# Recurrence and feed-forward kernel: a block's last decay fetched by small transfers in place of four matmuls, and another priority for the bias product

## Chip, cores, metric

One core of a Trainium2 chip. The metric is the device time in microseconds (us) of one execution; several executions are taken in rounds beside executions of the kernel before on the same chip. Runs in the slow state are left out of the ratios. The profile is one execution, with times from its first instruction on.

## The reference, cut

```python
f = 1.0 / (1.0 + np.exp(-f_logit))                 # q, k, v, f_logit: (4, 8, 768, 48)
for t in range(S):
    state = f[:, :, t, :, None] * state + np.einsum('bhd,bhe->bhde', k[:, :, t], v[:, :, t])
    y[:, :, t] = np.einsum('bhd,bhde->bhe', q[:, :, t], state)
x = y.transpose(0, 2, 1, 3).reshape(3072, 384)
h = x @ w_in                                       # 384 -> 2048
out = (np.maximum(h, 0) + np.log1p(np.exp(-np.abs(h)))) @ w_out   # 2048 -> 384
```

## The kernel before

Tokens come in 24 blocks of 128; six blocks make one sequence, and a 48x48 state per head is carried between them. In a block, ScalarE turns the gates into decays accumulated from the block's start (tile `ee`, tokens on partitions), POOL scales k and q by them (`qkp`), TensorE transposes and multiplies, and POOL updates the state (`sst`). The state needs the decay of the block's **last token**, a row on partition 127, as a column with one channel per partition. Four matmuls with a one-column selector (`last`) do that turn.

The feed-forward part of one block runs beside the recurrence of later blocks. All work is a list of tasks with a guessed cost and a key; a list scheduler simulates the engines and fixes the order of instructions per engine. On the chip an engine works its own list in order: SP's 192 issues in the trace of the changed kernel stand exactly as its list has them. All loads and stores are issued by SP.

```python
LOADS = 4                                    # load buffers per tensor
def in_order(tasks, slots): ...              # per engine: of the ready tasks the one that can start
                                             # first; at equal start the one with the lower key
def load(n, i):                              # n in f, k, q, v: 128 x 8 x 48 floats in 192-byte runs
    nc.sync.dma_start(out=t, in_=...)
def a_u(i):
    ...                                      # 4 matmuls 128x96: the block's k^T v
    for p in range(NP):                      # NP = 4 pairs of heads
        nc.tensor.matmul(out=ps[:, DM + p:DM + p + 1], lhsT=ek[:, p, :], rhs=last,
                         start=True, stop=True, skip_group_check=True)
def a_tt(i):
    ...                                      # tt = k^T v (+ old state)
    nc.vector.tensor_copy(out=ec, in_=ps[:, DM:DM + NP])
def a_sn(i):                                 # POOL: new state = tt * ec, twice, one per head of a pair
    nc.gpsimd.tensor_tensor(out=sn[lo:hi, :, e0:e0 + D], in0=tt[lo:hi],
                            in1=ec[lo:hi].unsqueeze(2).to_broadcast([48, NP, D]), op=ALU.mult)
# ... the tasks (engine, guessed cost in us, needs, key):
task(("go", n, i), "SP", 0.5, [(used[n], i - LOADS)], kd, load, (n, i))
task(("ek", i), "ACT", 0.48, [("cs", i)], s + 0.1, a_ek, (i,), "ee", [("mk", i), ("mq", i), ("u", i)])
task(("eq", i), "ACT", 0.48, [("ek", i)], s + 0.2, a_eq, (i,))
task(("bias mm",), "PE", 0.65, [("sum", len(sums) - 1)], NJ + LAG - 1, bias_mm, (), "att", [("bias out",)])
```

## Time and profile before

| | before |
|---|---|
| median of three runs, us | 200.12 (199.54 to 202.39) |
| span of the profiled run, us | 197.8 |
| TensorE idle between 57 and 195 us, sum of the gaps over 0.15 us, us | 0.72 |
| one block in the late part (mean of 9), us | 7.09 |
| granted TensorE clock | 1.00 |

The lines that carry this stand in the prediction. In the slices a digit is the busy share in tenths; the chain names at each moment the work on which the end depended; a bracket after a line of a timeline gives the idle time of that engine just before the instruction and who ended it.

### The profile page before, as it was taken

How to read it: one execution, taken by the hardware profiler on the slowest of the kernel's cores; microseconds unless marked ns; L12 is line 12 of the kernel's file. 1: busy time of each engine (PE TensorE's matmuls, PEld its weight loads, DVE VectorE, ACT ScalarE, POOL GpSimd, SP SyncE). 2: the span in 40 equal slices, each digit the busy share in tenths (PEclk: the TensorE clock that was granted, in tenths of full speed). 3: DMA queues.
4: the chain of work that ended last, by engine and by line, in shares of the span. 5: the costliest groups of instructions: out<-in, count | busy, mean ns of one | idle time of the engine just before them, and what ended most of it. 6: DMA issues, size and time to landing. Idle time of an engine off the chain costs nothing.

```text
span 197.8 us, 5863 instructions
## 1 busy us (share of the span) xinstructions
PE 181.5 (92%) x2354; PEld 147.9 (75%) x2354; DVE 127.8 (65%) x295; ACT 148.5 (75%) x247; POOL 97.4 (49%) x142
## 2 busy tenths in 40 slices
PE   0568898999979999999999999999999999999993
PEld 0345797777768888887788888888888888888871
DVE  6658977526949988667558657755855865773021
ACT  4446349899679899896898797898869768676870
POOL 2268747999998662460463364254246335400000
PEclk9999999999999999999999999999999999999999
DMA  6999999999999999999977657856441101100112
GB/s 127 188 187 215 352 389 373 208 201 166 196 169 202 206 203 196 246 186 199 203 155 165 120 134 150 159 118 136 114 85 41 43 0 43 40 14 29 43 40 80
DMA packets 107035, 30.26 MB, mean 153 GB/s; under 512 B 100352, under 2 KB 105472, under 8 KB 107008
## 3 DMA queue, kind: packets, MB, share of 16 engines
q1 hardware_dynamic: 107008, 29.89, 73.4%
q8 instruction: 18, 0.29, 0.7%
q14 instruction: 9, 0.07, 0.1%
HBM read 25.17 MB, written 4.72 MB: 151 GB/s over the span
## 4 chain that ended last, share of the span: by engine, by line
PE 64%; POOL 13%; SPq 9%; DMA 8%; issue 3%; ACT 2%; DVE 0%; POOLq 0%
PE ops L367 24%; PE hh L347 24%; SPq L111 8%; POOL wsum L177 7%; DMA w<-in_moe_w_out_dram 6%; PE qkT L232 4%; PE pp L257 4%; DMA ff<-in_f_logit_dram 2%; POOL w_out_bf L162 2%; PE oo L319 2%; PE xTp L333 2%; POOL qkp L214 1%; PE uu L274 1%; SPq L148 1%; PE cs L201 1%
## 5 line engine op out<-in xcount | busy, mean ns | idle before, releaser
L347 PE MATMUL hh<-xT,w_in_bf 128*128 128x128 bf16 x1152 | 118.2, 222 | 1.7 <-ACT uexp L355 1.6
L367 PE MATMUL ops<-w_out_bf,gg 128*128 128x384 bf16 x384 | 113.7, 326 | 0.0
L347 PEld LDWEIGHTS <-w_in_bf 128*128 128x128 bf16 x1152 | 92.0, 99 | 24.1 <-issue 2.8
L355 ACT ACTIVATE uexp<-hh 128x512 f32<-128x512 f32 x96 | 56.6, 594 | 26.1 <-PE hh L347 25.4
L361 ACT ACTIVATE gg<-uexp 128x1024 bf16<-128x1024 f32 x48 | 50.7, 1057 | 1.5
L303 POOL TENSOR_TENSOR sst<-tt,ec 48x192 bf16<-48x192 f32 x40 | 20.7, 517 | 44.4 <-DVE ec L295 36.6
L367 PEld LDWEIGHTS <-gg 128*128 128x128 bf16 x384 | 36.8, 98 | 3.8
L265 DVE TENSOR_TENSOR ptm<-pp,mask 128x512 bf16<-128x512 f32 x48 | 30.9, 684 | 2.8 <-PE pp L257 2.6
L214 POOL TENSOR_TENSOR qkp<-kk,ee 128x384 bf16<-128x384 f32 x23 | 21.3, 928 | 19.8 <-ACT ee L206 14.5
L239 DVE CAST xx<-oo 128x384 bf16<-128x384 f32 x21 | 11.7, 558 | 20.5 <-PE oo L319 20.3
L218 POOL TENSOR_TENSOR qkp<-qq,ee 128x384 bf16<-128x384 f32 x24 | 22.0, 915 | 5.0 <-ACT ee L210 4.9
L239 DVE COPY qkT<-qkT 128x512 bf16<-128x512 bf16 x24 | 10.1, 422 | 19.4 <-PE qkT L232 19.4
L232 PEld LDWEIGHTS <-qkp 128*128 128x128 bf16 x192 | 13.1, 104 | 8.6 <-DVE qkp L214 5.5
L232 PE MATMUL qkT<-ident,qkp 128*128 128x128 bf16 x192 | 16.9, 234 | 2.7 <-DVE qkp L214 1.5
L375 DVE TENSOR_TENSOR osb<-ops,bias_bc 128x384 f32<-128x384 f32 x20 | 11.1, 555 | 11.4 <-PE ops L367 11.1
L193 ACT ACTIVATE ff<-ff 128x384 f32<-128x384 f32 x24 | 12.2, 514 | 7.3 <-DMA ff<-in_f_logit_dram 7.3
L257 PE MATMUL pp<-qbd,qkT 112*128 112x256 bf16 x96 | 16.8, 292 | 0.5 <-DVE qbd L248 0.2
L177 POOL TENSOR_TENSOR wsum<-wsum,w 128x384 f32<-128x384 f32 x14 | 14.7, 1048 | 0.7
L206 ACT ACTIVATE ee<-cs 128x384 bf16<-128x384 f32 x24 | 11.4, 477 | 3.8 <-PE cs L201 1.6
L223 POOL CAST vb<-vv 128x384 bf16<-128x384 f32 x24 | 12.3, 517 | 2.4 <-DMA vv<-in_v_dram 1.4
L201 PE MATMUL cs<-zz,negU 128*128 128x384 bf16 x24 | 8.5, 353 | 5.4 <-ACT zz L197 5.4
L197 ACT ACTIVATE zz<-ff 128x384 bf16<-128x384 f32 x24 | 12.4, 516 | 0.3
(49 smaller groups left out, 174.6 us busy)
## 6 DMA issues: line engine op xcount, KB each, us to landing
ff<-in_f_logit_dram SPq DMA_DIRECT2D x24, 192.0 KB, 4.3
kk<-in_k_dram SPq DMA_DIRECT2D x24, 192.0 KB, 4.3
qq<-in_q_dram SPq DMA_DIRECT2D x24, 192.0 KB, 4.5
vv<-in_v_dram SPq DMA_DIRECT2D x24, 192.0 KB, 4.4
out_dram<-osb SPq DMA_DIRECT2D x24, 192.0 KB, 2.1
w<-in_moe_w_in_dram SPq DMA_DIRECT2D x4, 768.0 KB, 8.3
w<-in_moe_w_out_dram SPq DMA_DIRECT2D x4, 768.0 KB, 13.1
```

The source lines that it names most:

```text
L177: nc.gpsimd.tensor_tensor(out=wsum, in0=wsum, in1=t[:, j, :], op=ALU.add)
L214: eng.tensor_tensor(out=qkp_bufs[i % 3][:, H:2 * H, 0:D], in0=in_t.pop(("k", i)), in1=e_bufs[i % 2][:, H:2 * H, 0:D], op=ALU.mult)
L218: nc.gpsimd.tensor_tensor(out=qkp_bufs[i % 3][:, 0:H, 0:D], in0=in_t.pop(("q", i)), in1=e_bufs[i % 2][:, 0:H, 0:D], op=ALU.mult)
L232: nc.tensor.transpose(ps[:, a * 128:(a + 1) * 128], qkp[:, a, :], ident)
L239: nc.vector.tensor_copy(out=out, in_=in_)
L257: nc.tensor.matmul(out=ps[:, u * 256:(u + 1) * 256], lhsT=qkT_t[i][0:112, NP + p, :], rhs=qbd_bufs[i % 2][0:112, p, :], start=True, stop=True,
L265: nc.vector.tensor_tensor(out=ptm_t[i][:, 4 * half:4 * half + 4, :], in0=p_ps.pop((i, half)).rearrange("p (a t) -> p a t", t=128), in1=mas ...
L303: nc.gpsimd.tensor_tensor(out=sn[lo:hi, :, e0:e0 + D], in0=tt[lo:hi], in1=ec[lo:hi].unsqueeze(2).to_broadcast([48, NP, D]), op=ALU.mult)
L347: nc.tensor.matmul(out=h_ps[i, j // 4][:, j % 4, :], lhsT=w_in_bf[:, r, j * 128:(j + 1) * 128], rhs=xT_t[i][:, r, :], start=(r == 0), stop ...
L355: nc.scalar.activation(out=u_t[i, a // 2][:, 4 * (a % 2):4 * (a % 2) + 4, :], in_=h_ps.pop((i, a)), func=AF.Exp, bias=0.0, scale=1.0)
L361: nc.scalar.activation(out=g_t[i][:, 8 * a:8 * a + 8, :], in_=u_t.pop((i, a)), func=AF.Ln, bias=0.5, scale=0.5)
L367: nc.tensor.matmul(out=o_ps[i][:, 0:DM], lhsT=g_t[i][:, j, :], rhs=w_out_bf[:, j, :], start=(j == 0), stop=(j == NJ - 1), skip_group_check ...
```

## The change

Its intent: take 64 matmuls off TensorE, the bound, and let the DMA engines (full until about 100 us, idle later) turn the row into a column: one 2-byte element per partition, four transfers per block, from block 4 on. And the bias product gets a later key, so that TensorE should not wait for POOL's sums.

```diff
+EC = 4
@@ a_u
-        for p in range(NP):
-            nc.tensor.matmul(out=ps[:, DM + p:DM + p + 1], lhsT=ek[:, p, :], rhs=last, ...)
+        if i < EC:
+            for p in range(NP):
+                nc.tensor.matmul(out=ps[:, DM + p:DM + p + 1], lhsT=ek[:, p, :], rhs=last, ...)
+    def a_ec(i):
+        ec_t[i] = work.tile([128, NP], BF16, name="ecd", tag="ecd", bufs=2)
+        row = e_bufs[i % 2][127:128, 0:H, :].rearrange("o (a b) d -> o a (b d)", b=2)
+        for p in range(NP):
+            nc.sync.dma_start(out=ec_t[i][:, p:p + 1], in_=row[:, p, :],
+                              allow_slow_non_contiguous=True)
@@ a_tt
-        nc.vector.tensor_copy(out=ec, in_=ps[:, DM:DM + NP])
+        if i < EC:
+            nc.vector.tensor_copy(out=ec, in_=ps[:, DM:DM + NP])
@@ tasks
+            if i >= EC:
+                task(("goec", i), "SP", 2.0, [("eq", i)], 0, a_ec, (i,), "ecd", [("sn", i)])
+                task(("ec", i), ("landing ec", i), 2.6, [("goec", i)], 0)
-            task(("u", i), "PE", 0.28, ...)
+            task(("u", i), "PE", 0.28 if i < EC else 0.17, ...)
-    task(("bias mm",), "PE", 0.65, [...], NJ + LAG - 1, bias_mm, ...)
+    task(("bias mm",), "PE", 0.65, [...], NJ + LAG + 8, bias_mm, ...)
```

More of the change, by code (lines that the diff above doesn't have):

```diff
@@ L224, in a_vb @@
                               in_=in_t.pop(("v", i)))
+    ec_t = {}
     qkT_ps, p_ps, u_ps, o_at, xT_ps, tt_t = {}, {}, {}, {}, {}, {}
@@ L276, in a_u @@
                              skip_group_check=True)
+        if i < EC:
+            for p in range(NP):
+                nc.tensor.matmul(out=ps[:, DM + p:DM + p + 1], lhsT=ek[:, p, :], rhs=last,
+                                 start=True, stop=True, skip_group_check=True)
+        u_ps[i] = ps
+    def a_ec(i):
+        ec_t[i] = work.tile([128, NP], BF16, name="ecd", tag="ecd", bufs=2)
+        row = e_bufs[i % 2][127:128, 0:H, :].rearrange("o (a b) d -> o a (b d)", b=2)
         for p in range(NP):
-            nc.tensor.matmul(out=ps[:, DM + p:DM + p + 1], lhsT=ek[:, p, :], rhs=last,
-                             start=True, stop=True, skip_group_check=True)
-        u_ps[i] = ps
+            nc.sync.dma_start(out=ec_t[i][:, p:p + 1], in_=row[:, p, :],
+                              allow_slow_non_contiguous=True)
     def a_tt(i):
@@ L286, in a_tt @@
         tt = work.tile([128, NP, D], FP32, name="tt", tag="tt", bufs=2)
-        ec = work.tile([128, NP], FP32, name="ec", tag="ec", bufs=2)
+        ec = ec_t.pop(i) if i >= EC else work.tile([128, NP], FP32, name="ec", tag="ec", bufs=2)
         for lo, e0 in ((0, 0), (64, D)):
@@ L423 @@
         task(("ek", i), "ACT", 0.48, [("cs", i)], s + 0.1, a_ek, (i,), "ee",
-             [("mk", i), ("mq", i), ("u", i)])
+             [("mk", i), ("mq", i), ("u", i), ("ec", i)])
         task(("eq", i), "ACT", 0.48, [("ek", i)], s + 0.2, a_eq, (i,))
@@ L443 @@
         if c < NC - 1:
-            task(("u", i), "PE", 0.28, [("vb", i), ("tr", i)], s + 12, a_u, (i,), "att",
+            if i >= EC:
+                task(("goec", i), "SP", 2.0, [("eq", i)], 0, a_ec, (i,), "ecd", [("sn", i)])
+                task(("ec", i), ("landing ec", i), 2.6, [("goec", i)], 0)
+            task(("u", i), "PE", 0.28 if i < EC else 0.17, [("vb", i), ("tr", i)], s + 12, a_u, (i,), "att",
                  [("tt", i)])
-            task(("tt", i), "DVE", 0.88, [("u", i), ("sn", i - 1) if c else None], s + 12.1,
+            task(("tt", i), "DVE", 0.88 if i < EC else 0.73, [("u", i), ("ec", i), ("sn", i - 1) if c else None], s + 12.1,
                  a_tt, (i,))
@@ L478 @@
         task(("sum", n), "POOL", 0.91, [("at", "wo", w), ("sum", n - 1)], 36 + n, add_w, (w, j))
-    task(("bias mm",), "PE", 0.65, [("sum", len(sums) - 1)], NJ + LAG - 1, bias_mm, (), "att",
+    task(("bias mm",), "PE", 0.65, [("sum", len(sums) - 1)], NJ + LAG + 8, bias_mm, (), "att",
          [("bias out",)])
@@ L485 @@
         t.frees.extend(by[n] for n in t.until if n in by)
-    slots = dict(att=4, hh=2, ops=2, zz=2, ee=2, qkp=3, vb=3, qkT=2, qbd=2, ptm=2, xx=2, xT=6, uexp=3, w32=8,
+    slots = dict(att=4, hh=2, ops=2, zz=2, ee=2, qkp=3, vb=3, qkT=2, qbd=2, ptm=2, xx=2, xT=6, ecd=2, uexp=3, w32=8,
                  gg=6, osb=6)
```

## The prediction

> **What bounds the kernel now.** I read the page from the top: engine shares, the forty slices, the chain that ended last, then the timeline around what the diff touches.
>
> ```profile
> PE 181.5 (92%) x2354; PEld 147.9 (75%) x2354; DVE 127.8 (65%) x295; ACT 148.5 (75%) x247; POOL 97.4 (49%) x142
> ...
> PE   0568898999979999999999999999999999999993
> POOL 2268747999998662460463364254246335400000
> DMA  6999999999999999999977657856441101100112
> ...
> PE 64%; POOL 13%; SPq 9%; DMA 8%; issue 3%; ACT 2%; DVE 0%; POOLq 0%
> ```
>
> The reader is to see three stages. Up to about 57 us the chain runs through the loads and then POOL, which casts weights and adds the rows of the second weight matrix (15 sums of about 1 us). From 57 us to 194.5 us TensorE is full; a slice is 4.9 us. The DMA engines are full too, but only until about 100 us. The share of matmul time alone would prove little, since matmuls overlap; what proves the stage is the timeline of TensorE: between 60 and 190 us it lists only two idle gaps:
>
> ```profile
> 92.89 0.33 PE L347 MATMUL hh<-xT,w_in_bf 128*128 128x128 bf16 x3 [0.24 <-ACT uexp L355]
> 95.22 0.33 PE L347 MATMUL hh<-xT,w_in_bf 128*128 128x128 bf16 x3 [0.48 <-ACT uexp L355]
> ```
>
> Behind these 0.72 us stands ScalarE, which just before had waited for a gate load (ff), in the stretch where the DMA engines are full:
>
> ```profile
> 91.83 0.52 ACT L193 ACTIVATE ff<-ff 128x384 f32<-128x384 f32 x1 [1.75 <-DMA ff<-in_f_logit_dram]
> ```
>
> So after 57 us a matmul removed from the order is time saved one for one, unless another engine or the loads hold that stage.
>
> **What the Trainium skill says.** (1) "TensorE: Matmul & The Clock Gate", section "Back-to-back issue gap": a matmul with 1 to 64 moving columns costs an issue floor of about 25 ns, not its latency. The trace agrees: four of the removed matmuls occupy 0.105 us, worked out below, 26 ns each, though each record is 163 to 205 ns long. (2) "DMA: Bandwidth & Descriptors", section "Anatomy of one DMA — SWDGE (gpsimd) path" (written for the other issuing path): about 2 us per transfer are fixed, mostly completion; and the engines do not wait on semaphores, the issuing sequencer does, before dispatch. The trace agrees: a store takes 2.1 us to land, and SP sits in front of stores for 60.3 us in its own list of waits. (3) Same page, section "Rules for kernel authors": a strided or non-contiguous last dimension becomes one descriptor per element. No run shows this yet; I expect 128 descriptors of 2 bytes per small transfer.
>
> **The change part by part.** *Which blocks.* There are 24 blocks, the state is carried after all but every sixth, so 20 have a decay; blocks 0 to 3 keep the old way. Sixteen change: 4, 6 to 10, 12 to 16, 18 to 22.
>
> *Removed from TensorE:* four matmuls (128x1) in each of them. The steady order of the timeline gives the cost as the distance of two starts:
>
> ```profile
> 111.43 0.33 PE L274 MATMUL uu<-vb,qkp 128*128 128x96 bf16 x4
> 111.60 0.24 PE L278 MATMUL uu<-last,ee 128*128 128x1 bf16 x4
> 111.71 0.32 PE L367 MATMUL ops<-w_out_bf,gg 128*128 128x384 bf16 x1
> ```
>
> 111.71 - 111.60 = 0.11, and other blocks give 0.10 to 0.11, so 0.105 us. 16 x 0.105 = 1.7 us. Block 4 lies before 57 us, where POOL leads; 15 blocks remain, 1.6 us. Ten of these (12 to 16, 18 to 22) come after 95 us, where nothing but TensorE counts: 1.05 us are safe. The 0.5 us of blocks 6 to 10 fall in the stretch with full DMA engines and may be lost.
>
> *Removed from VectorE:* 16 copies of 163 ns, 2.6 us, of an engine that is 65% busy and at 0% of the chain: nothing.
>
> *Added on SP and the DMA engines:* 64 transfers of 128 descriptors. A store, also of 128 descriptors, holds SP for 0.36 us when the queue is free, and the next issue can start some 0.1 us later; four of them are an estimated 1.8 us of SP per block. A block now has four loads and a store, 4 x 0.45 + 0.45 = 2.3 us of issue in a period of 7.0 us when the queue is free, so there is room late in the kernel. In the full stretch one load takes 0.98 us for 1024 descriptors, that is 64 on each of 16 engines, 15 ns each. At that rate 512 more descriptors per block are 32 x 15 ns = 0.5 us; 2-byte writes may be dearer. Blocks 4 and 6 to 10 are six blocks, 3 us of additional queue before 95 us, or more if SP's waiting holds the loads up.
>
> *Does the value arrive in time?* The state update on POOL (sst) reads it. In the steady state of block 14:
>
> ```profile
> 107.71 0.48 ACT L210 ACTIVATE ee<-cs 128x384 bf16<-128x384 f32 x1
> ...
> 113.62 1.08 POOL L303 TENSOR_TENSOR sst<-tt,ec 48x192 bf16<-48x192 f32 x2 [3.44 <-DVE ec L295]
> 115.09 0.91 POOL L214 TENSOR_TENSOR qkp<-kk,ee 128x384 bf16<-128x384 f32 x1 [0.39 <-DMA vv<-in_v_dram]
> ```
>
> The exponentials end at 108.19, and POOL wants them at 113.62: 5.4 us. The path is 4 issues, 1.8 us, and the landing, 2.1 us as for a store: 3.9 us, so 1.5 us of slack. If it were late, POOL would first eat the 0.4 us before the next product and then about 0.4 us in front of the transposes. In the full stretch loads land in 4.3 us, which makes 6.1 to 7 us against 6.7 (block 8), 6.4 (9) and 6.1 (10): about even, a few tenths lost at most per block.
>
> *Moved: the bias product.* Before, TensorE waits for the sums just there:
>
> ```profile
> 56.59 0.91 PE L183 MATMUL biasps<-wsum,ones 128*128 128x384 f32 x2 [1.34 <-POOL wsum L177]
> ```
>
> It is tempting to book these 1.34 us as gain. I counted the matmuls before this position: the first product of row block 4 had reached column tile 11, key 75. In the scheduler a lower key goes first among what is ready. The key changes from 16 + 24 - 1 = 39 to 16 + 24 + 8 = 48, and every other TensorE task still open then has a key of 66 (transposes of block 6) or more. Old or new, the product is the first choice once the scheduler thinks the sums are done. So I expect it to stay where it is, and the wait with it, unless the other changes shift it. And if it did move: the next transposes at 58.67 us wait for POOL's product, which ends at 58.28 and could begin only when the sums had ended, so most of the wait would only move there. I book 0 to 0.5 us, 0.2 in the middle.
>
> *Sum:* -1.6 for the matmuls, -0.2 for the bias, +0.8 for loads that come later before 95 us and for values that land late: -1.0 us on the 200.12 us of the runs. I predict 199.1.
>
> **The rivals.** *A, full credit:* both gains hold, -1.6 - 1.3 = -2.9 us, 197.2 us. For it speaks that TensorE is full after 57 us; against it the keys, POOL's pace, and the stretch before 95 us. *B, the loads are pushed back:* SP issues in order, so loads now stand behind small transfers that wait for exponentials. The gate load that ScalarE needed at 91.83 was issued at 87.98 and is late already; 2 to 3 us more would reach TensorE almost whole, +2.5 - 1.3 = +1.2 us, 201.3 us. For it: full DMA engines for 100 us, SP issuing without a break from 38 to 95 us. Against it: the new costs make the scheduler order the gate exponentials anew, and it may put that one later. *C, the landing becomes the new wait in every block:* were 2-byte transfers to take 3 us longer than a store, POOL would be late by 1.5 us and the transposes by 0.7 us in ten blocks, +7 - 1.6 = +5.4 us, 205.5 us. For it speaks only that no transfer of this kind has been measured here; against it the 1.5 us of slack.
>
> **Range and chances.** A to B spans 197.2 to 201.3; the new costs also reshuffle the whole order from block 4 on, which I cannot work out and count as one microsecond either way. So 197.0 to 201.6. Faster by over 2% needs under 196.1, more than the removed work is worth: 0.05. Slower by over 2% needs over 204.1, rival C or a bad B: 0.07. Within 2%: 0.88.
>
> **What would show it right or wrong.** Right: 16 (not 80) columns of this small matmul left on TensorE, the steady period shorter by 0.1 us; small transfers landing in 2 to 3 us late in the kernel, 4 or more before 95 us; the bias product with the same neighbours and about the same wait; ScalarE waiting as long or longer for gate loads around 85 to 100 us; POOL's state update hardly ever waiting for a DMA after 100 us. Wrong: a bias product without a wait and TensorE ahead by over 1 us at 65 us (A); idle gaps on TensorE of over 2 us between 60 and 100 us (B); a wait of POOL for the small transfers in every block, with TensorE idle before the transposes (C).

## The result, and the profile after

The changed kernel took 212.53 us (median of four runs, 211.44 to 213.13), the one before 200.46 in the same rounds: ratio 1.058, interval 1.049 to 1.068, slower. A ratio here is the mean time of one kernel's fast runs over that of the other's fast runs of the same rounds, so not quite the ratio of the medians quoted.

The page of the changed kernel (engine shares; slices of 5.2 us; chain by engine; one line of the DMA issues: name, count, size, us from issue to landing):

```profile
PE 183.7 (88%) x2290; PEld 147.7 (70%) x2290; DVE 125.9 (60%) x279; ACT 147.9 (71%) x247; POOL 98.5 (47%) x142
...
PE   0568888999439999929999999999999999999993
...
PEclk9999999999955999996999999999999999999999
...
PE 65%; POOL 10%; SPq 10%; DMA 8%; ACT 3%; issue 2%; DVE 0%; POOLq 0%; ACTq 0%
...
ecd<-ee SPq DMA_DIRECT2D x64, 0.2 KB, 2.1
```

The 64 matmuls are gone (2290 in place of 2354). TensorE has holes that were not there before, in the slices from 52 to 63 us and around 90 us, and its clock falls to half behind them. The transfers land in 2.1 us, quicker than the loads. From its timeline, the gaps of TensorE after 50 us:

```profile
57.91 0.48 PE L325 MATMUL oo<-sst,qkT 112*128 112x96 bf16 x4 [3.21 <-POOL sst L314]
...
62.66 1.65 PE L184 MATMUL biasps<-wsum,ones 128*128 128x384 f32 x2 [3.06 <-POOL wsum L178]
...
93.15 0.40 PE L234 MATMUL qkT<-ident,qkp 128*128 128x128 bf16 x4 [3.30 <-POOL qkp L215]
94.02 0.40 PE L234 MATMUL qkT<-ident,qkp 128*128 128x128 bf16 x4 [0.47 <-POOL qkp L219]
```

All are waits for POOL, and POOL waited for a value of the small transfers. Behind the gaps at 93 and 94 us stands this line of POOL, for block 9:

```profile
91.03 1.08 POOL L314 TENSOR_TENSOR sst<-tt,ecd 48x192 bf16<-48x192 f32 x2 [7.28 <-DMA ecd<-ee]
```

Block 4, from the timelines of ScalarE, SP and POOL in this order:

```profile
42.58 0.48 ACT L211 ACTIVATE ee<-cs 128x384 bf16<-128x384 f32 x1
...
50.08 0.93 SPq L112 DMA_DIRECT2D qq<-in_q_dram  x1
51.10 0.92 SPq L112 DMA_DIRECT2D ff<-in_f_logit_dram  x1
52.12 3.03 SPq L289 DMA_DIRECT2D ecd<-ee  x4
55.24 0.54 SPq L112 DMA_DIRECT2D kk<-in_k_dram  x1
...
56.78 1.08 POOL L314 TENSOR_TENSOR sst<-tt,ecd 48x192 bf16<-48x192 f32 x2 [6.04 <-DMA ecd<-ee]
```

The exponentials are done at 43.06, and the transfers begin at 52.12: 9 us later, because they stand behind loads in SP's list and each load holds SP for about 0.9 us. The four issues then take 3.0 us. In the scheduler's own simulation the transfers start at 42.2, with one load issued since 21.9: it believes SP idle, since it books 0.5 us per load and knows nothing of the backlog. Behind POOL's late state update stand the four last sums, so the bias product waits 3.06 us in place of 1.34. ScalarE waits as well: the transfers read `ee`, which has two buffers, and at 56.73 us it had stood 4.78 us until they were done with one. The prediction has no such wait.

The half clock, seen in the table by stretch (busy us of PE, PEld, DVE, ACT, POOL with counts; then granted clock, DMA share, GB/s):

```profile
58.00:60.00 2.00, 1.51 (x16) 0.89 (x15) 0.56 (x1) 1.97 (x4) 1.92 (x3) 0.50 1.22 203
...
63.00:66.00 3.00, 3.00 (x20) 2.21 (x20) 1.62 (x3) 0.38 (x1) 3.00 (x5) 0.50 0.72 128
...
94.00:97.00 3.00, 2.98 (x27) 2.35 (x28) 2.15 (x6) 0.24 (x1) 0.41 (x1) 0.65 1.12 189
```

The trace's clock records give half clock from 57.37 us on for 10.24 us and from 94.91 us on for 3.41 us.

**Where the 11.9 us between the two spans lie.** The listed gaps of TensorE after its start-up (from 20 us on) add up to 12.6 us after and 3.5 us before; from 40 us on, to 10.25 and 2.06 us, so +8.2 us. Of the 13.65 us at half clock TensorE worked in about 10, which costs half of that, 5.0 us (an estimate from the table by stretch). The matmuls removed give 1.7 us back. 8.2 + 5.0 - 1.7 = 11.5 us. All of it is lost before 118 us: the cumulative sum of block 14 starts at 105.88 before and at 118.51 after, the one of block 23 at 169.73 and 181.56. The nine blocks between take 63.85 and 63.05 us, so the changed kernel is indeed 0.09 us faster per block there.

**What SP does** in the two stretches, before and after. The table by stretch of the kernel before:

```profile
52.00:95.00 43.00, 41.17 (x586) 34.56 (x585) 32.63 (x78) 36.26 (x63) 25.44 (x36) 1.00 1.09 200
105.00:140.00 35.00, 35.00 (x489) 29.31 (x487) 23.69 (x58) 29.45 (x51) 15.20 (x23) 1.00 0.68 142
```

and of the one after:

```profile
52.00:95.00 43.00, 32.67 (x414) 26.74 (x412) 25.78 (x56) 26.98 (x47) 22.88 (x32) 0.88 0.86 154
105.00:140.00 35.00, 35.00 (x478) 29.24 (x477) 23.75 (x53) 29.81 (x52) 15.21 (x23) 1.00 0.73 132
```

In the early stretch the DMA engines fall from 1.09 to 0.86 of their time (the share adds up the packets' times, so it can pass 1), though there is more to transfer: they now wait for SP. Adding up the issues in SP's timeline (duration of each issue inside the stretch; a merged row counts from its first start to its last end; a load begun just before 52 us is counted in):

| 52 to 95 us | SP issuing, share | loads issued | small transfers issued, us of SP |
|---|---|---|---|
| before | 0.89 | 36 | 0 |
| after | 0.91 | 28 | 22, 14.2 us |

Before, SP's issues were long (0.9 us for a load on average, where 0.37 is the least), which I put down to the DMA engines being behind; now they are many. In the same time eight loads, two blocks' worth, are missing.

### The profile page after: what moved, and what is told of

The parts are those of the page before. It is cut to its first block, busy times and chain, and to the rows that moved or that the text cites. A ratio compares the mean times of both kernels' runs of the same rounds, so it can differ in the third digit from the quotient of the medians.

```text
span 209.7 us, 5844 instructions
## 1 busy us (share of the span) xinstructions
PE 183.7 (88%) x2290; PEld 147.7 (70%) x2290; DVE 125.9 (60%) x279; ACT 147.9 (71%) x247; POOL 98.5 (47%) x142
## 4 chain that ended last, share of the span: by engine, by line
PE 65%; POOL 10%; SPq 10%; DMA 8%; ACT 3%; issue 2%; DVE 0%; POOLq 0%; ACTq 0%
PE ops L378 25%; PE hh L358 24%; SPq L112 7%; DMA w<-in_moe_w_out_dram 6%; POOL wsum L178 5%; PE qkT L234 4%; PE pp L259 4%; DMA ecd<-ee 2%; SPq L289 2%; POOL w_out_bf L163 2%; PE oo L330 2%; PE xTp L344 1%; PE cs L202 1%; SPq L149 1%; PE uu L276 1%
## 5 line engine op out<-in xcount | busy, mean ns | idle before, releaser
L378 PE MATMUL ops<-w_out_bf,gg 128*128 128x384 bf16 x384 | 114.9, 328 | 1.1 <-POOL w_out_bf L163 1.1
L314 POOL TENSOR_TENSOR sst<-tt,ecd 48x192 bf16<-48x192 f32 x32 | 16.4, 514 | 57.8 <-DMA ecd<-ee 21.9
L378 PEld LDWEIGHTS <-gg 128*128 128x128 bf16 x384 | 37.3, 98 | 5.4 <-issue 1.6
L234 PE MATMUL qkT<-ident,qkp 128*128 128x128 bf16 x192 | 17.8, 238 | 6.9 <-POOL qkp L215 3.3
L211 ACT ACTIVATE ee<-cs 128x384 bf16<-128x384 f32 x24 | 11.6, 484 | 4.8 <-DMA ecd<-ee 4.8
L207 ACT ACTIVATE ee<-cs 128x384 bf16<-128x384 f32 x24 | 11.5, 478 | 4.9 <-PE cs L202 3.2
L241 DVE COPY xT<-xTp 128x384 bf16<-128x384 bf16 x21 | 7.5, 355 | 11.5 <-PE xTp L344 11.5
```

The costliest lines, as they stand in the source:

```text
L234: nc.tensor.transpose(ps[:, a * 128:(a + 1) * 128], qkp[:, a, :], ident)
L241: nc.vector.tensor_copy(out=out, in_=in_)
L378: nc.tensor.matmul(out=o_ps[i][:, 0:DM], lhsT=g_t[i][:, j, :], rhs=w_out_bf[:, j, :], start=(j == 0), stop=(j == NJ - 1), skip_group_check ...
```

## The experiments

I began with **theory Q** (position): the value comes late because the transfers stand too far back in SP's list; free the value and the time is back. Its rivals: **T**, each transfer costs time in every block; **L**, the transfers hold back the loads behind them; later **S**, the sharper form of L: SP's issue time is the resource, so that values and loads both come late; **D**, packets or descriptors cost, not issues; **O**, the new order of work is itself worse.

**The bias key alone.** Changing only this key, in the kernel before as in the one after, leaves the instruction lists of all five engines identical, row by row. So it needed no run: this part of the change does nothing.

**e1_from6.** `EC = 6`.

> Small transfers only from block 6 on (15 of 16 kept; block 4 keeps the matmuls). Theory Q (queue position): the value of block 4 reached POOL 9 us after its exponentials because its transfers stood behind loads on SP; that one block cost 3.2 + 3.1 us of idle TensorE before 63 us and about 9 us of half clock. Without it both gaps go, the old bias wait of about 1.3 us returns, a gap of about 3 us near 93 us (block 9) may stay: 201 to 205 us. Rival T (each small transfer costs time of its own, on SP or the DMA engines, in every block): 15 of 16 are still there, so about 211.5 us.

Measured 211.0 us, ratio 1.051 (1.045 to 1.057). A miss for Q: block 4's gaps are gone (the bias wait is 1.34 us again), and others came in their place: 1.30, 1.06 and 4.04 us of idle TensorE between 67 and 83 us, again at half clock behind them. The loss moves to the next block that uses the transfers.

**e2_from12.** `EC = 12`.

> Small transfers only from block 12 on (10 blocks), after the stretch in which SP issues loads without a break. Theory Q: the values arrive in time, no idle TensorE from them, 10 x 0.105 = 1.05 us fewer matmuls: 198.5 to 200 us against 200.5 before, ratio 0.990 to 0.999. Rival T: 10 of 16 of the loss of 12 us, about 208 us.

Measured 199.53 us, ratio 0.993 (0.986 to 0.9995), as expected. A block in the late part takes 7.00 us. So T falls as a cost in every block: ten blocks of transfers show none here, and the loss belongs to the stretch before about 95 us.

**e3_unread.** The matmuls compute the decay again; the transfers remain, from a constant, unread:

```diff
-        if i < EC:                        # matmuls, and the copy in a_tt
+        if True:
-        row = e_bufs[i % 2][127:128, 0:H, :].rearrange("o (a b) d -> o a (b d)", b=2)
+        row = mask4[127:128]
```

> Same order of work as the changed kernel, the same 64 transfers at the same places of SP's order, but copied from a constant tile, and nobody reads what they bring: the four matmuls and the copy are back and give the decay. Correct result. Theory Q: only the wait for the value costs; issue and traffic are free, so 199.5 to 202.5 us. Rival T or rival L (the transfers hold back the loads behind them): most of the 12 us remain, 207 us or more.

Measured 213.28 us, ratio 1.062 (1.057 to 1.067). **Q falls.** Nobody waits for what these transfers bring, and the whole loss is still there. It is now the loads that are late; from the timelines of POOL and of ScalarE in this kernel:

```profile
68.35 0.84 POOL L224 CAST vb<-vv 128x384 bf16<-128x384 f32 x1
77.83 0.51 POOL L224 CAST vb<-vv 128x384 bf16<-128x384 f32 x1 [8.64 <-DMA vv<-in_v_dram]
78.30 0.91 POOL L215 TENSOR_TENSOR qkp<-kk,ee 128x384 bf16<-128x384 f32 x1
...
111.13 0.52 ACT L194 ACTIVATE ff<-ff 128x384 f32<-128x384 f32 x1 [4.10 <-DMA ff<-in_f_logit_dram]
```

TensorE idles 4.94 us at 79 us behind the first and 3.76 us at 112 us behind the second, a gate load. I read the late value in the changed kernel as one face of the same thing.

**e4_act_queue.** `nc.scalar.dma_start` in place of `nc.sync.dma_start`, right after the exponentials.

> The same transfers issued by ScalarE right after the exponentials, no longer in SP's order. Theory Q: the values land about 2 us plus four issues after the exponentials, in blocks 4 to 10 as well, so the gaps at 58 and 93 us go; the price is ScalarE's issue time, 4 x 0.5 to 0.6 us, in a block of 7 us of which ScalarE is busy 5.3: near its limit, so 199 to 205 us. Rival T: gaps stay, 210 us or more.

Measured 237.48 us, ratio 1.185 (1.175 to 1.195), far outside Q's range (and in T's, 210 us or more: each block with transfers does pay here, on ScalarE). POOL waits for no value any more. The timelines of ScalarE and TensorE show what came in its place:

```profile
104.32 0.48 ACT L211 ACTIVATE ee<-cs 128x384 bf16<-128x384 f32 x1
104.83 2.98 ACTq L291 DMA_DIRECT2D ecd<-ee  x4
107.86 1.08 ACT L368 ACTIVATE uexp<-hh 128x512 f32<-128x512 f32 x2 [3.06 <-issue]
...
108.51 0.33 PE L360 MATMUL hh<-xT,w_in_bf 128*128 128x128 bf16 x3 [2.41 <-ACT uexp L368]
```

Four issues stop ScalarE's list for 2.4 to 3.0 us, and TensorE runs out of the exponentials (`uexp`) that stand behind them: 15 such gaps of 0.8 to 2.7 us, 29 us in all, one in nearly every block with transfers. A late block now takes 9.5 us, of which ScalarE works 5.7 and issues about 2.5, so I read the place of the issues in its list as the cost, not a full ScalarE. The issue time goes with the issue: ScalarE pays it here.

**e5_zero, e6_one_unread, e3_unread, e10_one_512: counting issues.** All four have the changed kernel's order of work, all matmuls and a right result; they differ in what SP issues per block.

```diff
# e5_zero: none
-        for p in range(NP):
-            nc.sync.dma_start(...)
# e6_one_unread: one of 128 elements
+        row = mask4[127:128]
+        nc.sync.dma_start(out=ec_t[i][:, 0:1], in_=row[:, 0, :], allow_slow_non_contiguous=True)
# e10_one_512: one of 128 x 4 elements, each 2 bytes by itself (ec_t twice as wide)
+        row = mask4[:, :, 0:1]
+        nc.sync.dma_start(out=ec_t[i].rearrange("p (a b) -> p a b", b=2)[:, :, 0:1], in_=row, allow_slow_non_contiguous=True)
```

> The order of work of the changed kernel with all matmuls back and none of the 64 transfers. Control of e3_unread. Theory S (SP's issue time is the cost: four issues hold SP 2.4 to 4 us per block, in a stretch where SP issues without a break, so values and loads both come late): 200 to 203 us, as before or a little worse by the shuffled order. Rival O (the new order of work itself is bad, whatever SP does): 208 us or more.

> As e3_unread, with one transfer per block in place of four, at the same places of SP's order; nobody reads it. Theory S: SP loses 0.6 to 1 us per block in place of 2.4 to 4, about a quarter of what e3_unread lost against e5_zero: 202 to 206 us. Rival D (one such transfer in flight is enough to disturb the loads behind it): 208 us or more.

> As e6_one_unread, one transfer per block that nobody reads, but of 128 x 4 separate 2-byte elements of a constant: as many 2-byte packets as the four transfers of e3_unread, in one issue. If SP's time goes by issues (theory S), 200.5 to 203.5 us, like e6_one_unread. If by packets or descriptors, like e3_unread: 209 to 214 us.

| kernel | issues x elements per block | median, us | ratio to before (95%) | DMA share 52 to 95 us | loads issued there |
|---|---|---|---|---|---|
| e5_zero | 0 | 199.03 | 0.993 (0.990 to 0.996) | 0.99 | 36 |
| e6_one_unread | 1 x 128 | 201.36 | 1.003 (0.995 to 1.011) | 0.95 | 34 |
| e10_one_512 | 1 x 512 | 202.74 | 1.010 (1.004 to 1.016) | 0.94 | 32 |
| e3_unread | 4 x 128 | 213.28 | 1.062 (1.057 to 1.067) | 0.80 | 27 |

The runs come from three chips; the kernel before took 201.0 to 201.1 us beside each. The rows by stretch of e5_zero, e10_one_512 and e3_unread, in this order:

```profile
52.00:95.00 43.00, 41.57 (x594) 34.89 (x593) 33.87 (x79) 37.48 (x66) 26.98 (x38) 1.00 0.99 196
```

```profile
52.00:95.00 43.00, 41.69 (x593) 34.88 (x592) 33.80 (x80) 37.56 (x65) 26.43 (x37) 1.00 0.94 177
```

```profile
52.00:95.00 43.00, 36.17 (x500) 30.05 (x498) 29.57 (x70) 31.02 (x54) 24.05 (x35) 0.96 0.80 146
```

The order of work (O) is not to blame: without transfers it is even 0.7% faster than before. Against one issue of 128 elements, four times the packets in one issue take 1.4 us more, which is within the noise (the intervals overlap); the same packets in four issues take 10.5 us more than in one. So D is a small part at most, and S stands: the number of issues decides. Two things stay unseparated: each issue is also a transfer with a completion of its own, and e10_one_512 reads its elements from 128 partitions, e3_unread from one (their 2-byte packets take 8.3 and 7.6 ns on average, so the packets themselves are not dearer in e3_unread). An issue of 128 elements holds SP for 0.47 us at the least, of 512 for 0.605. The cost is not proportional (2.3 us for one issue, 14.3 for four); I take it that late loads meet engines that work in order, and in e3_unread the clock falls at the two longest waits.

**e7_costs and its control e8_before_costs.** The scheduler is told how long SP's issues take:

```diff
-task(("go", n, i), "SP", 0.5, ...)                 # f, k, q, v
+task(("go", n, i), "SP", 0.5 if i < LOADS else 0.95, ...)
-task(("go", n, i), "SP", 0.5, ...)                 # weights
+task(("go", n, i), "SP", 0.5 if n == "wi" else 6.5, ...)
```

> The changed kernel, with the scheduler's costs of an issue on SP set to what the trace before shows (0.95 us for a load after block 3 in place of 0.5; 6.5 us for a load of the second weights), so that it places the transfers and the loads knowing how far SP lags. Theory Q+S (position and issue time on SP): values no longer late by 5 to 7 us, so 200 to 206 us. If only issue time matters and position not: 209 us or more.

> Control of e7_costs: the kernel before with the same costs in the scheduler. Expected close to before: 198 to 203 us.

e7_costs measured 212.05 us, ratio 1.058 (1.053 to 1.062), and its control 202.64 us, 1.012 (1.008 to 1.016). Another miss for position: block 4's transfers now start at 46.4 us, and no gap of TensorE after 57 us is longer than 1.4 us, yet the time is the same. The loss has spread: ScalarE waits for gate loads 14 times. Two lines of the list of waits (who waited for whom, us in total, times, longest):

```profile
POOL sst L314 <- DMA ecd<-ee: 24.9, 6, 5.6
ACT ff L194 <- DMA ff<-in_f_logit_dram: 17.9, 14, 3.2
```

Here both values and loads are late: this other order of SP's list moves the loss and does not remove it.

**e11_pool_queue.** `nc.gpsimd.dma_start`, after POOL's product with q.

> The four transfers issued by POOL, after its product with q, all 16 blocks; SP's order as without them. POOL has about 3.5 us free in a block of 7. Theory S: loads are no longer held back; what it costs is POOL's issue time. If four issues take POOL under 3 us, late blocks hold and the time is 197.5 to 202 us, early blocks (POOL full until 62 us) lose 1 to 2 us; if 4 us or more, POOL becomes the bound and it is 205 us or more.

Measured 208.03 us, ratio 1.035 (1.029 to 1.041), against 1.058 on SP. Four issues take POOL 2.16 us, under the 3 us that I had set, but the time is outside the range given for that. POOL is full until 62 us and delays its casts (`vb`), for which TensorE idles 2.14, 1.65 and 1.47 us at 48, 63 and 68 us; later 1.89 us at 126 us, where the value lands late. Loads are better off (33 issued from 52 to 95 us). A third engine, and again a price, 7 us, in another place.

**e9_order_from12 and e12_order_from18: looking for a version that beats both.** The changed kernel's order, with the transfers from block 12 or 18 on and matmuls before.

> The changed kernel's order of work (which alone, in e5_zero, ran at 0.993 of before), with the transfers only from block 12 on, where SP is issuing about 40% of the time; blocks 0 to 10 keep the matmuls. Theory S: e5_zero's 199.0 us less 10 x 0.105 = 1.05 us: 197.5 to 198.7, ratio 0.983 to 0.990, faster than both kernels. If late transfers cost something too: 199 us or more.

> As e9_order_from12, with the transfers only in blocks 18 to 22, when hardly any load is left to issue (the last is issued near 135 us). Theory S: nothing stands behind the transfers, no new gaps on TensorE, so e5_zero's 0.993 of before less 5 x 0.105 = 0.5 us: ratio 0.987 to 0.994, about 198.5 us. If a transfer costs time even with an idle SP: 0.996 or more.

e9_order_from12: 199.16 us, ratio 0.996 (0.991 to 1.0007), a miss: the saving is eaten by small gaps of TensorE, 1.6 us in four from 102 to 119 us, and SP is issuing 0.91 of the time from 105 to 140 us, where e5_zero has 0.40. e12_order_from18: 199.02 us, ratio 0.993 (0.989 to 0.996), in the range expected; TensorE has no gap after 103 us, but 0.5 us of saving is too small to tell from e5_zero's 0.993. e2_from12 with its own order shows no such loss while SP issues 0.80 of that time, so a busy SP alone does not settle it: in e9_order_from12 the transfers of blocks 12 to 16 begin 2.6 to 3.6 us after their exponentials, in e2_from12 at most 0.4 us. Where transfers cost nothing here, they save a microsecond at most. The fastest here are e2_from12, e5_zero and e12_order_from18, all at 0.993 and not to be told apart; e5_zero has no transfer at all, so most of what they gain may be the order of work.

## Why the prediction was wrong, point by point

The prediction was 199.1 us, between 197.0 and 201.6; the runs gave 212.53.

- **The matmuls, -1.6 us: right.** Late blocks are 0.09 us shorter; 0.105 us for each block with a decay was expected, and eight of these nine have one.
- **The bias product: right.** The key is without effect; the new order as a whole moved the product by one column tile (nine of row block 4 before it, ten in the kernel before), and it waits longer because POOL is later. The key given for the tile then due is off by one, 74 and not 75; nothing hangs on it.
- **The landing: right late in the kernel, too cautious in the full stretch.** 2.1 us at the median and 4.1 at most over all 64, where I feared 4.3 before 95 us.
- **"The path is 4 issues, 1.8 us, and the landing": the step that failed first.** It lets SP begin when the exponentials end. In the full stretch SP began 4.4 to 9.1 us later; late in the kernel, 0.0 to 1.3 us later, and there the path holds. The in-order list of SP had been noted in rival B, but only as something that delays loads.
- **"3 us of additional queue before 95 us": the mis-sized term.** I priced the transfers by the time of the DMA engines, 0.5 us per block. That was even too much: a 2-byte packet takes 7.5 ns on average, so 0.24 us per block. What they take is SP's time, 2.4 to 3.2 us per block in place of the 1.8 that I had worked out and then booked only where SP was free. SP issuing without a break from 38 to 95 us stood in my own text; from it I should have expected added issues to push the later loads back. The six early blocks took 16.1 us of SP; eight of 36 loads were missing. In the sum all this was the +0.8 us for late loads and values, a figure with no working behind it: the spans lie 11.9 us apart with 1.7 us of matmuls removed, so the term came to some 13.6 us (an estimate).
- **The clock was not in the sum at all.** Half clock began at the end of the gap of 3.21 us and after that of 3.30 us, and cost about 5 of the 11.9 us (the estimate above).
- **The rivals.** B had the mechanism and a tenth to a fifth of the size, and its sign, gaps of over 2 us between 60 and 100 us, came true (3.06 and 3.30 us). But ScalarE's waits for gate loads, B's path, fell from 7.3 to 5.6 us: in the changed kernel the late values show first. The -1.3 us in B's sum is not worked out. C was judged by the landing, not by the queue. Both rest on one resource, which the experiments name: taking away the wait (e3_unread) or moving the transfers (e7_costs) leaves the loss, putting the same packets into one issue (e10_one_512) takes most of it away, and taking away the issues (e5_zero) all of it.
- **The range.** A to B with one microsecond either way is 196.2 to 202.3 us, not 197.0 to 201.6; 212.53 lies outside both.
- **Open:** how the loss splits between late values and late loads in the changed kernel itself, since removing one uncovers the other; and the share of the clock, which no run isolates.

## What to carry to other kernels

Price a transfer in three currencies: bytes on the DMA engines, latency to landing, and the time that its issue holds an in-order engine; four tiny transfers move next to nothing and still cost an issuer 2.2 us or more. Before adding issues to a queue, add up that queue's issues in the stretch concerned, as for any other engine, since SP can be the bound although it computes nothing. When a change of order is meant to help, compare the instruction lists first: a key that changes no order needs no run.

## What the Trainium skill lacked or had wrong

- "DMA: Bandwidth & Descriptors", section "Issuing engines are not separate DMA queues", calls the sequencer's time to initiate a DMA "usually small relative to the DMA itself". For small transfers it is not: an issue held SP 0.47 to 0.6 us where the whole transfer landed in 2.1 us, ScalarE about 0.6 us and POOL 0.53 us; 64 of them on SP cost 14.3 us of time (e3_unread against e5_zero), on ScalarE 37 us. The page gives no measured trn2 time for which one issue holds its engine; it has 512 cycles per instruction for "previous generations" in a passage on a later chip.
- Same page, section "Rules for kernel authors", one descriptor per element for a non-contiguous last dimension: confirmed on SP, 8192 packets of 2 bytes for 64 transfers (issued from POOL, e11_pool_queue, the trace has 1024 packets of 16 bytes). This row warns of the layout, and another row of the same table says to coalesce many small transfers; neither gives the issuer's share. Here 512 such elements in one issue cost 3.7 us over none and 128 in each of four issues 14.3 us, so the number of issues weighs more.
- "TensorE: Matmul & The Clock Gate", section "Part 1: The HAM clock gate", agrees in the window: the half clock lasted 10.24 and 3.41 us in the changed kernel, multiples of the 3.4 us that it gives. It differs, or is too coarse, in what ends full clock. It says "after ≥1 idle window (~3.4µs)", yet over all runs here the clock fell 17 times, and in the 3.41 us before each fall TensorE was not idle throughout but busy for 0.2 to 1.52 us; in e7_costs it was busy for 1.49 us, with no gap over 0.72 us. Of the windows of that length, counted from the clock records, that kept full clock, one had 1.48 us of work and all others 1.52 or more. So gaps that add up to over half of a window were enough here.
- No page lists the issue time of a 192 KB load under backlog: 0.37 us at the least when the queue was free, 0.9 us on average from 52 to 95 us.
